# Attention with a bucketed position bias and a gated feed-forward block on one core: another opening (turns as plain products, one-step bias table, bias rows in 16 copies, another order)

## The chip, the cores and the metric

The kernel runs on one core of one Trainium2 chip. The core has five engines with an instruction queue each: TensorE (PE, matrix products into PSUM), VectorE (DVE), ScalarE (ACT), GpSimd (POOL) and SyncE (SP, which here only issues transfers). ACT and POOL issue transfers as well. All transfers share 16 DMA engines. PSUM has 8 banks of 128 x 512 fp32. The metric is device time in microseconds (us), lower is better.

## The reference

Inputs are q, k, v of shape 8 x 8 x 576 x 64 (batch, heads, positions, head size), a bias table of 32 x 8, and a feed-forward layer with w_in 512 x 2048, w_out 2048 x 512 and alpha 2048, all fp32. What is computed:

```
scores = q k^T / 8 + bias_table[bucket(|i - j|)]     # one bias per head and distance
attn   = softmax(scores);   x = (attn v), heads side by side: 4608 x 512
h = x w_in;   s = sin(alpha h);   g = h + s*s / (alpha + 1e-9);   out = g w_out
```

The bucket is the distance itself below 16, grows with its logarithm up to 31, and is 31 for every far distance.

## The kernel before, in words

Work goes batch by batch (t = 0 to 7). For each batch the scores are made transposed, keys on partitions: two heads of a pair share a product, four blocks of 128 keys (units "A", 128 x 1024 each) and a last 64 keys (unit "C"); the last 64 queries are units "B" and "X", which for batch 0 are done beside batch 1. ACT takes exp(scores / 8) from PSUM into the tile u (L707). The bias is not added but multiplied in afterwards, as exp(bias): since exp of the bias of the last bucket is a common factor that the softmax cancels, the table is taken relative to its last row, and then only a band of some 384 queries around each block of keys needs the product (DVE, L738, by the tile m2r; the C units by mhr, L724). After that u is multiplied by v with a column of ones beside it (products with v and vh), DVE divides by the sums (L952, L953), the result is turned on PE (L1024) and copied to xT, the input of the feed-forward layer. There 16 blocks of 128 columns go through w_in, sine (ACT, L1068), square (ACT L1075 or DVE L1077) and the sum (DVE, L1082) into g; products with w_out follow, and are used to fill PE where the next batch's scores wait for ACT. ACT loads another function table between exponentials and sines (L1146).

The order of instructions on each engine is made when the program is built, by a list planner written in the kernel (class Plan): each task has a priority, an estimated length per engine and sometimes an earliest time (the constants T_...), and the planner emits tasks in the order in which its own clock would run them. On the chip only that order counts; engines wait for each other by semaphores. Where the planner sees PE idle early on, it puts in products of a tile of zeros (zz).

The opening is special. For batch 0, q and k are loaded in their own layout: pair 0 of heads into nat0 (SP, fp32, cast to natb by DVE and POOL, L467, L515, L516), pairs 1 to 3 into nat1 (POOL, cast on the way). They are turned on PE by transposes with the identity (L550, L556: 6 or 12 of 96 columns for one of k or q of one pair) into one PSUM bank as fp16, and copied by DVE into kT and qT (L539). The last 64 keys are copied once more into kt by POOL (L581).

The bias rows are made in the same stretch (plan_table): a fp32 product with a matrix that subtracts the last row of the table (less, L592), its exponential (tabE, L595), a product with the 0/1 bucket constant phi (8 x 512), a copy to e_sb (L605), a transfer of e_sb to DRAM in 5 copies (e_dram, L606), and reads of these back into the 128 partitions, each shifted by one element: m2r in three transfers (2, 2 and 4 heads), mhr in two.

v of batch 0 comes in two ways: heads 0, 1 and 4 to 7 in fp32 by SP into a corner of w_out's tile, cast by POOL (L422); heads 2, 3 and the last 64 keys by POOL's own casting transfers (L414, L426). POOL then issues w_in (four transfers, each two of four row blocks of half the columns; a copy of one element of m2r, named tick, makes it wait for the last band), q and k of batch 1 (nat2), w_out, and v of batch 1.

Of the kernel before, what the change touches and what calls it, by code (L numbers as in the profile page):

```python
# [36 lines left out]
PAIRS = ((0, 1), (2, 3), (4, 5))  # L37
BANKS = {"h": (0, 1, 2, 3, 4, 5), "av": (6, 7), "mo": (7, 6)}


class Task:
    def __init__(self, engs, emit, deps, pri, nb=0.0):
# [5 lines left out]
        self.pad = ()  # L48
# [9 lines left out]
class Cell:  # L58
    v = None


class Plan:
# [31 lines left out]
    def pick(self, b, taken):  # L94
        sets = PAIRS if b.tag == "sc" else [(k,) for k in BANKS[b.tag]]
# [53 lines left out]
    def run(self, t0):  # L149
        free = {e: t0 for e in ("PE", "ACT", "DVE", "POOL", "SP")}  # L150
        todo = list(self.tasks)
        while todo:
# [33 lines left out]
            if e == "PE" and WARM_FROM < free[e] < WARM_END and st > free[e] + WARM_GAP:  # L186
                if self.fill(free[e], 192):
                    free[e] += 0.083
                    continue
# [15 lines left out]
            for n in t.pad if fin < WARM_END else ():  # L205
                self.fill(fin, n)
# [4 lines left out]
WARM_END = 22.0  # L211
# [3 lines left out]
T_START = 4.0  # L215
SPLIT = {0: 3, 1: 3}
PRI_S = 0
T_WI = 16.8
T_TAB = 5.2
T_CL = 24.5  # L220
T_FIRST = (4.75, 5.95)
T_PAIR = ((7.9, 8.5), (9.3, 10.2), (11.6, 12.3))
T_ACT = ()
T_M2 = (13.0, 14.8, 16.0, 16.0)
T_MH = 14.2
T_RST = 25.0
T_V0 = (5.8, 6.4, 8.9, 9.6)
T_P3 = 7.0
T_VA = (10.5, 11.0)
T_VB = (19.5, 19.5, 19.5, 19.5)  # L230
T_AL = (10.0, 560)
LATE = 100
GA = 0.1
# [8 lines left out]
T_V = ((15.5, 19.0), (50.0, 50.0))  # L242
T_TR1 = (36.0, 39.0)
T_W = (25.5, 30.5)
T_WO = (40.5, 43.0, 45.7, 48.3)
WARM0 = 8
WARM1 = 2
WARM_LAG = 0.3
WARM_GAP = 0.12
WARM_FROM = 7.3  # L250
AV_PRI = 400
NORM_PRI = 200
CP_PRI = 0
SIN_SET = "trig_and_small"
# [15 lines left out]
def kernel(  # L270
# [26 lines left out]
    NE = 5  # L297
# [12 lines left out]
    for x in range(EW - 1):  # L310
        phi_np[bt[abs(x - 255)], x] = 1.0
    last_np = np.eye(NB, dtype=np.float32)
    last_np[NB - 1] -= 1.0
    phi_h = nc.inline_tensor(np.concatenate([phi_np, last_np.view(np.float16)], axis=1), "phi_const")
# [16 lines left out]
        "p (h c d) -> p h c d", h=H, c=4)  # L331
    zz = sgl.tile([128, 512], F16, name="zz")
# [5 lines left out]
    tabE = sgl.tile([NB, H], F16, name="tabE")  # L338
    phi_x = sgl.tile([NB, EW + 2 * NB], F16, name="phi_sb")
    phi_sb, less_last = phi_x[:, 0:EW], phi_x[:, EW : EW + 2 * NB].bitcast(F32)  # L340
# [72 lines left out]
    def load_vh(t, h):  # L413
        nc.gpsimd.dma_start(  # L414
            out=vs[t][:, :, h, 0:D], in_=v[t, h, 0:512].rearrange("(c p) d -> p c d", p=128)
        )

    def load_v32(h):
        nc.sync.dma_start(out=vst[:, h], in_=v[0, h, 0:512].rearrange("(c p) d -> p c d", p=128))

# [809 lines left out]
```

## Time and profile before

Three runs took 372.21, 372.88 and 376.88 us (median 372.88). The profiled execution is one more; its own time is given only as its span, from the first to the last instruction.

| | profiled execution before |
|---|---|
| span | 374.9 us (run time around it not shown) |
| PE busy | 368.2 us (98%) |
| ACT busy | 315.7 us (84%) |
| DVE busy | 257.8 us (69%) |
| POOL busy | 91.9 us (25%) |
| first exponential on ACT | 9.11 us |
| first sine | 34.98 us |
| first product with w_out | 49.79 us |

A row of the timeline gives the start, the length, the engine, the line, the operation with its tiles (written <- read), its shape and how many were merged; in brackets stands the idle time before it and what ended it. "issue" means that nothing in the profile explains the wait. A busy PE is not PE at its best: the products of zeros count as busy, and so does a product that runs slowly. Rows of transfers give the number, the KB of each and the median us from issue to landing.

### The profile page before, as it was taken

To read this page: it belongs to the slowest core of one execution; us is meant where nothing else is said; L and a number is where in the kernel's file an instruction comes from. 1 tells how busy PE (TensorE), PEld (TensorE's weight loads), DVE (VectorE), ACT (ScalarE), POOL (GpSimd) and SP (SyncE) were. 2 spreads that over 40 slices of the span, in tenths; PEclk is the share of its full clock that TensorE was granted. 3 is DMA by queue.
4 is the path that set the end of the run, shared out by engine and by line. 5 is a ranking of instruction groups with operands and counts; after the bars stand their busy time and mean duration, and the time that the engine had idled before them with its cause. 6 is when DMAs were issued, how large, how long until landed. Compare 5 with 4: busy or idle time off the path is not lost.

```text
span 374.9 us, 8925 instructions
## 1 busy us (share of the span) xinstructions
PE 368.2 (98%) x3576; PEld 197.4 (53%) x3576; DVE 257.8 (69%) x559; ACT 315.7 (84%) x431; POOL 91.9 (25%) x133
## 2 busy tenths in 40 slices
PE   8999999999999999999999999999999999999996
PEld 3455454644455455684564455444576455444443
DVE  3496976759676967597758867786759675879000
ACT  2787989979997999899989999799979997999211
POOL 7368270037000640055002800090006000000000
PEclk9999999999999999999999999999999999999999
DMA  9969999369922998199917992699249121000112
GB/s 168 201 113 192 200 173 160 83 112 112 133 64 62 151 143 123 48 160 137 133 48 134 125 168 58 122 88 187 59 111 118 65 58 47 7 27 5 73 69 85
DMA packets 149114, 40.49 MB, mean 108 GB/s; under 512 B 137080, under 2 KB 143568, under 8 KB 149072
## 3 DMA queue, kind: packets, MB, share of 16 engines
q0 software_dynamic: 96032, 17.67, 58.3%
q1 hardware_dynamic: 52864, 22.16, 24.6%
q8 instruction: 28, 0.46, 0.5%
q10 hardware_dynamic: 176, 0.09, 0.1%
q14 instruction: 14, 0.11, 0.1%
HBM read 37.73 MB, written 16.56 MB: 145 GB/s over the span
## 4 chain that ended last, share of the span: by engine, by line
PE 95%; ACT 3%; DVE 1%; issue 0%; ACTq 0%
PE pb L457 92%; ACT u L707 3%; PE pb L556 2%; PE pb L1024 1%; PE pb L550 0%; DVE xn L953 0%; DVE u L738 0%; DVE qT L539 0%; DVE zz L508 0%; ACT outs L537 0%; ACT xT L537 0%; DVE rd L952 0%; PE pb L646 0%; PE pb L934 0%; ACTq L537 0%
## 5 line engine op out<-in xcount | busy, mean ns | idle before, releaser
L707 ACT ACTIVATE u<-pb 128x1024 f16<-128x1024 f32 (+1 forms) x146 | 137.4, 1017 | 11.9 <-PE pb L457 10.5
L457 PE MATMUL pb<-w_out,g 128*128 128x512 f16 (+2 forms) x592 | 139.0, 374 | 0.0
L457 PE MATMUL pb<-xT,w_in 128*128 128x512 f16 (+4 forms) x704 | 127.4, 340 | 0.0
L1082 DVE SCALAR_TENSOR_TENSOR g<-sq,inv_a,pb 128x512 f16<-128x512 f16 x144 | 101.3, 744 | 7.1 <-PE pb L457 2.7
L1068 ACT ACTIVATE s<-pb,alphaT 128x512 f16<-128x512 f32 x144 | 92.9, 692 | 12.4 <-PE pb L457 11.9
L457 PEld LDWEIGHTS <-w_in 128*128 128x128 f16 x704 | 64.6, 98 | 57.4
L457 PEld LDWEIGHTS <-g 128*128 128x128 f16 x592 | 53.9, 98 | 60.2 <-issue 5.6
L738 DVE TENSOR_TENSOR u<-u,m2r 128x512 f16<-128x512 f16 (+1 forms) x128 | 62.3, 493 | 33.6 <-ACT u L707 31.9
L457 PEld LDWEIGHTS <-u 128*128 128x128 f16 x1152 | 43.4, 97 | 9.6 <-issue 4.6
L402 POOL COPY kt<-kT 64x256 f16<-64x256 f16 x12 | 4.9, 410 | 172.0 <-DMA kT<-staged_k 107.8
L457 PE MATMUL pb<-qT,kT 64*128 64x64 f16 (+1 forms) x512 | 43.3, 293 | 1.1 <-ACT u L707 0.6
L1075 ACT ACTIVATE sq<-s 128x512 f16<-128x512 f16 x69 | 43.1, 637 | 1.2 <-DVE g L1082 0.3
L457 PE MATMUL pb<-v,u 128*128 128x65 f16 x1024 | 43.7, 193 | 0.0
L1077 DVE TENSOR_TENSOR sq<-s 128x512 f16<-128x512 f16 x75 | 30.9, 422 | 12.5 <-ACT s L1068 11.7
L953 DVE TENSOR_TENSOR xn<-pb,rd 128x256 f16<-128x256 f32 (+2 forms) x59 | 28.5, 483 | 2.0
L457 PEld LDWEIGHTS <-kT 64*128 64x128 f16 x512 | 16.2, 95 | 23.1 <-issue 16.8
L457 PE MATMUL pb<-vh,u 128*128 128x130 f16 x128 | 28.2, 221 | 0.0
L407 POOL DMA_DIRECT2D v<-in_v_dram x28 | 24.8, 900 | 4.0 <-DMA nat<-in_k_dram 2.1
L537 ACT ACTIVATE outs<-pb 128x512 f32<-128x512 f32 (+2 forms) x12 | 6.9, 572 | 19.9 <-PE pb L457 19.9
L952 DVE RECIPROCAL rd<-pb 128x4 f32<-128x4 f32 (+2 forms) x59 | 11.0, 186 | 13.3 <-PE pb L457 13.1
L539 DVE COPY outs<-pb 128x512 f32<-128x512 f32 x25 | 17.2, 686 | 4.1 <-PE pb L457 4.1
L1146 ACT ACT_TABLE_LOAD x15 | 19.2, 1283 | 0.3
(75 smaller groups left out, 192.5 us busy)
## 6 DMA issues: line engine op xcount, KB each, us to landing
out_dram<-outs SPq DMA_DIRECT2D x35, 256.0 KB, 2.8
v<-in_v_dram POOLq DMA_DIRECT2D x28, 128.0 KB, 4.6
staged_k<-in_k_dram POOLq DMA_DIRECT2D x6, 576.0 KB, 8.9
staged_q<-in_q_dram POOLq DMA_DIRECT2D x6, 576.0 KB, 12.1
w_in<-in_moe_w_in_dram POOLq DMA_DIRECT2D x4, 512.0 KB, 8.5
w_out<-in_moe_w_out_dram POOLq DMA_DIRECT2D x4, 512.0 KB, 14.5
w_out<-in_v_dram SPq DMA_DIRECT2D x6, 128.0 KB, 5.7
xT<-xn SPq DMA_TRANSPOSE x47, 2.4
```

The lines of the kernel that those rows point to most:

```text
L407: nc.gpsimd.dma_start(out=vs[t % 2][:, c, :, 0:D], in_=vp[128 * c : 128 * c + 128],)
L457: nc.tensor.matmul(out=out, lhsT=lhsT, rhs=rhs, start=start, stop=stop)
L539: k_of(e).tensor_copy(out=o, in_=i)
L707: nc.scalar.activation(out=o, in_=x, func=AF.Exp, scale=0.125)
L738: nc.vector.tensor_tensor(out=io, in0=io, in1=m2[:, 2 * p : 2 * p + 2, x0 : x0 + hi - lo], op=ALU.mult)
L952: nc.vector.reciprocal(out=r, in_=x[:, :, :, D])
L953: nc.vector.tensor_tensor(out=xn[:, 0:n].rearrange("p c (z d) -> p c z d", z=2), in0=x[:, :, :, 0:D], in1=r.unsqueeze(3).to_broadcast([128 ...
L1068: nc.scalar.activation(out=s16.v, in_=h.v, func=AF.Sin, scale=alphaT[:, f : f + 1])
L1075: nc.scalar.activation(out=sq.v, in_=s16.v, func=AF.Square)
L1077: k_of(e).tensor_tensor(out=sq.v, in0=s16.v, in1=s16.v, op=ALU.mult)
L1082: nc.vector.scalar_tensor_tensor(out=gcell[b].v[:, f, :], in0=sq.v, scalar=inv_a[:, f : f + 1], in1=h.v, op0=ALU.mult, op1=ALU.add,)
L1146: nc.scalar.preload_act_table_set(name)
```

## The change

All of it concerns batch 0 and the loads around it.

- The turns of batch 0 become plain matrix products with the identity. Their result is fp32 and takes two PSUM banks (three blocks of 96 columns in each), from four possible bank pairs of which three are those of the scores. DVE copies out of the two banks.
- The table: DVE splits the fp32 table into two fp16 parts (tab16), before its casts of q and k; two products with phi add up the parts, and phi itself carries the -1 for the last row. ACT takes the exponential straight from PSUM into e_sb. The fp32 product and its exponential are gone.
- e_sb is written to DRAM in 16 copies instead of 5; a band (m2r) is read head by head, eight transfers, partitions spread over the copies in groups of 8.
- nat0 is loaded in halves, one head each, on SP and on ACT; phi and alpha move from ACT's queue to SP's. The last cast of q of pair 0 moves from POOL to ACT.
- v: all heads and the last 64 keys now come in fp32 by SP and are cast by POOL.
- POOL's queue: w_in in three transfers by columns (a quarter, a quarter, a half), after the casts of v of heads 2, 3 and 4 and without the tick; then the other casts, q and k of batch 1, and w_out after all casts.
- Zeros: 7 products of 512 and 6 of 128 columns at the start, and fewer later; other times and lengths in the planner, and a table of priorities (HEAD_PRI) for the first tasks.

The order that results: PE makes the turns of pair 0, then both turns of pair 1, then the first two score units. On SP stand, after the first loads: bands 0 and 1, the two of mhr, bands 2 to 7, v of heads 2 to 7. In the feed-forward block of batch 0, 48 products with w_in stand before the first turn of batch 1 (40 before), and 12 products with w_out before the first scores of batch 1 (17 before). Later batches are ordered much as they were.

```diff
-    last_np = np.eye(NB, dtype=np.float32)
-    last_np[NB - 1] -= 1.0
-    phi_h = nc.inline_tensor(np.concatenate([phi_np, last_np.view(np.float16)], axis=1), "phi_const")
+    phi_np[NB - 1, 0 : EW - 1] -= 1.0
+    phi_h = nc.inline_tensor(phi_np, "phi_const")
...
-    load_nat(nat0[:, 0], 0, 2, k[0], nc.sync)
-    load_nat(nat0[:, 1], 0, 2, q[0], nc.sync)
     nc.scalar.dma_start(out=tabN, in_=bias_table)
-    nc.scalar.dma_start(out=phi_x, in_=phi_h.ap())
-    nc.scalar.dma_start(out=alphaN, in_=moe_alpha.rearrange("(f p) -> f p", p=128))
+    for kq, src in ((0, k), (1, q)):
+        for z, eng in ((0, nc.sync), (1, nc.scalar)):
+            load_nat(nat0[:, kq, z : z + 1], z, z + 1, src[0], eng)
+    nc.sync.dma_start(out=phi_sb, in_=phi_h.ap())
+    nc.sync.dma_start(out=alphaN, in_=moe_alpha.rearrange("(f p) -> f p", p=128))
     load_v32(0)
     load_v32(1)
+    load_vt32()
...
-    cast0(0, nc.vector)
-    x0 = nat0[:, 1].rearrange("s two (i d) -> s i two d", i=SI)
-    nc.vector.tensor_copy(out=natb[:, 1, :, 0], in_=x0[:, :, 0])
-    P_.tensor_copy(out=natb[:, 1, :, 1], in_=x0[:, :, 1])
+    nc.vector.tensor_copy(out=tab16[:, 0], in_=tabN)
+    nc.vector.tensor_tensor(out=tab16[:, 1], in0=tabN, in1=tab16[:, 0], op=ALU.subtract)
+    x0 = nat0.rearrange("s kq two (i d) -> s kq i two d", i=SI)
+    for kq, z in ((0, 0), (0, 1), (1, 0)):
+        nc.vector.tensor_copy(out=natb[:, kq, :, z], in_=x0[:, kq, :, z])
+    nc.scalar.activation(out=natb[:, 1, :, 1], in_=x0[:, 1, :, 1], func=AF.Copy)
...
         def mm(e):
+            if t == 0:
+                c.v = bank(b, 2)
+                for i in range(SI):
+                    o = c.v[:, i // 3, SN * (i % 3) : SN * (i % 3) + SN]
+                    if p == 0:
+                        full(o, natb[:, kq, i], id_sb[0:SN, 0:SN], True, True)
+                        continue
+                    for z in range(2):
+                        full(o[64 * z : 64 * z + 64], nat1[:, kq, 2 * p - 2 + z, D * i : D * i + D],
+                             id_sb[0:SN, 0:SN], True, True)
+                return
...
+        def mm(e):
+            for x in range(2):
+                full(bank(b)[0:H, 0:EW], tab16[:, x], phi_sb, x == 0, x == 1)
 
         def ex(e):
-            nc.scalar.activation(out=tabE, in_=bank(a)[0:NB, 0:H], func=AF.Exp)
...
+            nc.scalar.activation(out=e_sb, in_=bank(b)[0:H, 0:EW], func=AF.Exp)
+            nc.scalar.dma_start(out=e_dram.ap()[:, 0:H].rearrange("r h x -> h r x"),
+                                in_=e_sb.unsqueeze(1).to_broadcast([H, NE, EW]))
+            load_m2r(0, 2)
             load_mhr(nc.sync)
...
+    def load_m2r(h0, h1):
+        n = 128 // NE
+        for h in range(h0, h1):
+            nc.sync.dma_start(
+                out=m2r[:, h],
+                in_=bass.AP(tensor=e_dram, offset=EW * h, ap=[[4 * H * EW + n, NE], [1, n], [1, XW]]),
+            )
...
-        def w_in(e):
-            P_.tensor_copy(out=tick, in_=m2r[0:1, 4, 0:1])
-            for hf in range(2):
-                load_w_in16(hf, (0, 2))
...
+        for h in range(H):
+            vdone.append(plan.add({"POOL": 0.45}, lambda e, h=h: cast_v(h), [], 9010 + h, nb=T_V0[h]))
...
+        x = vdone[2]
+        for i, (x0, x1) in enumerate(((0, 1), (1, 2), (2, 4))):
+            x = plan.add({"POOL": 0.85}, lambda e, x0=x0, x1=x1: load_w_in16(x0, x1), [], 9012.5 + i,
+                         nb=T_WI + 0.8 * i, after=[x])
+        x = plan.add({"POOL": 1.7}, lambda e: load_nat2(), [], 9021, nb=T_RST, after=[x])
+        x = plan.add({"POOL": 3.2}, lambda e: load_w_out16(), [], 9022, nb=T_WL, after=[x] + vdone)
...
+    for i, x in HEAD_PRI.items():
+        plan.tasks[i].pri = x
     plan.run(T_START)
```

More of the change, by code (lines that the diff above doesn't have):

```diff
@@ L149, in run @@
     def run(self, t0):
-        free = {e: t0 for e in ("PE", "ACT", "DVE", "POOL", "SP")}
+        free = dict(t0)
         todo = list(self.tasks)
@@ L611, in cp, with bands @@
+            load_m2r(0, 2)
             load_mhr(nc.sync)
[L612 to L614 removed]
+        def bands(e):
+            load_m2r(2, H)
+            for h in range(2, H):
                 load_v32(h)
[L617 to L618 removed]
+        x = plan.add({"PE": D_TAB}, mm, [], -1100, nb=T_PHI, new=[b])
+        y = plan.add({"ACT": 1.1}, ex, [x], -1100, use=[b])
@@ L726, in bd @@
                 )
-            d = plan.add({"POOL": 0.45} if t == 0 and p else {"DVE": 0.25 if two else 0.15}, bd, [x],
+            d = plan.add({"POOL": 0.6} if t == 0 and p else {"DVE": 0.25 if two else 0.15}, bd, [x],
                          base + 10, nb=late, use=[ub])
```

177 lines of the change are left out of this document (77 added, 100 removed), and 10 rows, old and new, of the table HEAD_PRI.

## The prediction

> **What bounds the kernel now.** I read the summary page first: the span and the chain that ended last.
>
> ```profile
> span 374.9 us, 8925 instructions
> PE 95%; ACT 3%; DVE 1%; issue 0%; ACTq 0%
> ```
>
> PE holds 95% of the chain, so later work moves earlier only if the opening (the first 51 us, which the diff rewrites) hands it over earlier. A busy PE says little there, because part of its work is products of zeros and part runs slowly. The timeline shows the pace:
>
> ```profile
> 1.27 3.92 PE L457 MATMUL pb<-zz 128*128 128x512 f16 x10 [1.27 <-DVE zz L508]
> 33.92 7.50 PE L457 MATMUL pb<-xT,w_in 128*128 128x512 f16 x34
> 19.08 0.39 PE L457 MATMUL pb<-zz 128*128 128x256 f16 x1
> 20.80 0.30 PE L457 MATMUL pb<-zz 128*128 128x256 f16 x1
> 8.47 0.61 PE L457 MATMUL pb<-qT,kT 64*128 64x512 f16 x2 [0.37 <-DVE qT L539]
> 21.13 0.39 PE L457 MATMUL pb<-qT,kT 64*128 64x512 f16 x2
> 11.15 0.69 PE L556 MATMUL pb<-id_sb,nat 96*64 96x96 f16 x12
> 41.35 0.45 PE L556 MATMUL pb<-id_sb,nat 96*64 96x96 f16 x12
> ```
>
> The first row is eight products of 512 columns and two of 192: 4480 columns in 3.92 us, 1.14 per ns. The second is 17408 in 7.50 us, 2.32 per ns. The same zero product falls from 0.39 to 0.30 us between 19.08 and 20.80, a score pair from 0.61 to 0.39, twelve turns from 0.69 to 0.45. In this execution PE ran at half pace until about 20.8 us. What that costs is read on ACT:
>
> ```profile
> 9.11 1.02 ACT L707 ACTIVATE u<-pb 128x1024 f16<-128x1024 f32 x1 [1.46 <-PE pb L457]
> 30.62 1.28 ACT L1146 ACT_TABLE_LOAD   x1
> 34.98 1.84 ACT L1068 ACTIVATE s<-pb,alphaT 128x512 f16<-128x512 f32 x3 [0.48 <-PE pb L457]
> 50.70 1.28 ACT L1146 ACT_TABLE_LOAD   x1
> 54.84 6.78 ACT L707 ACTIVATE u<-pb 128x1024 f16<-128x1024 f32 x7 [0.64 <-PE pb L457]
> ...
> L707 ACT ACTIVATE u<-pb 128x1024 f16<-128x1024 f32 x16 | 15.6, 1039 | 4.6 <-PE pb L457 4.6
> L707 ACT ACTIVATE u<-pb 128x512 f16<-128x512 f32 x4 | 2.4, 610 | 0.7 <-PE pb L457 0.7
> ```
>
> The last two rows group the twenty exponentials between 9 and 31 us (after the bar: busy time and mean ns of one; idle time before them and who ended it). After the first one ACT waits 4.6 + 0.7 - 1.46 = 3.84 us for PE. It reaches the sine at 34.98 and leaves feed-forward block 0 at 50.70 (second table load). Third, the transfers:
>
> ```profile
> 20.00:22.50 2.50, 2.47 (x38) 1.33 (x33) 2.50 (x7) 2.45 (x3) 2.41 (x5) 1.00 0.00 0
> 21.28 2.92 POOL L438 DMA_DIRECT2D w_in<-in_moe_w_in_dram  x4
> nat<-in_q_dram POOLq DMA_DIRECT2D x1, 576.0 KB, 10.0
> 32.13 0.78 POOL L432 DMA_DIRECT2D nat<-in_q_dram  x1
> 42.69 0.31 PEld L556 LDWEIGHTS <-nat 96*64 96x64 f16 x12 [0.42 <-issue]
> ```
>
> In the windows view the last two columns are DMA share and GB/s: nothing moves from 20.0 to 22.5, then w_in starts a queue (w_in, next batch's k and q, w_out, v) without a gap. Its q lands at 32.13 + 10.0 = 42.1, and PE begins turning it at 42.69, 0.6 later. So the start of w_in, W = 21.28, is a second chain beside ACT's: q at W + 20.8.
>
> **The change part by part.** *Turns.* As many products as before, into fp32, two PSUM banks instead of one. Why the pace rose at 20.8 no row says; the stretches before it had the same kinds of product with waits between (0.37 ahead of 8.47), and the new order sets more products back to back. If PE is at full pace when the exponentials begin, twelve cost 0.45 instead of 0.69, and a turn with a score pair 0.45 + 0.39 = 0.84 us, under an exponential's 1.02; at half pace it is 1.30, over it. The copy out now reads fp32:
>
> ```profile
> L539 DVE COPY qT<-pb 128x576 f16<-128x576 f16 x4 | 3.0, 755 | 3.1 <-PE pb L556 2.0 <-PE pb L550 1.1
> L539 DVE COPY outs<-pb 128x512 f32<-128x512 f32 x25 | 17.2, 686 | 4.1 <-PE pb L457 4.1
> ```
>
> The fp32 row scales to 0.686 x 576/512 = 0.77 us against 0.755: eight times 0.02, nothing. The extra banks can hold up a score pair: between 0 and one copy, 0.77; I take 0, since the exponentials leave a bank pair every 1.02. One bound of the other kind, a gain, is excluded: no copy gets shorter.
>
> The Trainium skill's "TensorE: Matmul & The Clock Gate" (Part 4) says that transpose-mode products do not count as PE-busy for the clock's release. Here 24 turns at 17.98 to 19.15 stood in the stretch after which the pace rose, so the trace neither bears this out nor excludes it. By that rule and the page's 3.4 us window, plain products would bring the release by about 8 us, an estimate; without it the half pace may last, which is a rival below.
>
> *Opening order.* Two turns of pair 1 now precede the first scores, so these wait for its q (issued 2.29, below; landing 6.1: 8.4). Turn 0.45 to 0.69 and scores 0.39 to 0.61 put the first exponential at 9.3 to 9.7 instead of 9.11; I take +0.4. Three xT copies instead of one now stand on ACT before the table load (+0.76), and fewer after it. The exponentials end at 30.62 - 3.84 + 0.40 + 0.76 = 27.9.
>
> *Table.* The fp32 subtraction and its exponential go, two tiny DVE operations and a second 512-column product come.
>
> ```profile
> 2.29 0.64 POOL L432 DMA_DIRECT2D nat<-in_q_dram  x1
> nat<-in_q_dram POOLq DMA_DIRECT2D x3, 144.0 KB, 6.1
> phi_sb<-phi_const ACTq DMA_DIRECT2D x1, 36.0 KB, 4.0
> 6.44 0.58 PE L457 MATMUL pb<-phi_sb,tabE 32*8 32x512 f16 x1
> 7.06 0.59 ACT L605 ACTIVATE e_sb<-pb 8x512 f16<-8x512 f32 x1 [0.67 <-PE pb L457]
> 7.68 0.52 ACTq L606 DMA_DIRECT2D e_dram<-e_sb  x1
> 10.28 0.37 SPq L473 DMA_DIRECT2D m2r<-e_dram  x1
> 10.69 1.34 SPq L480 DMA_DIRECT2D mhr<-e_dram  x2
> m2r<-e_dram SPq DMA_DIRECT2D x2, 192.0 KB, 4.4
> mhr<-e_dram SPq DMA_DIRECT2D x2, 96.0 KB, 4.3
> w_out<-in_v_dram SPq DMA_DIRECT2D x6, 128.0 KB, 5.7
> ```
>
> The constant is third on SP (about 1.7) and lands at 1.7 + 4.0 = 5.7; products of 0.43 + 0.58 end at 6.7, and e_sb starts 0.3 us earlier than 7.06. The write grows from 40 to 128 KB. Written and acknowledged it took 10.28 - 7.68 = 2.6; the bounds are that and the 4.3 of a 96 KB landing. I take 2.9, which eats the 0.3: the first band read stays at 10.3. The Trainium skill's "DMA: Bandwidth & Descriptors" (Rules for kernel authors) says that a transfer whose outermost dimension is under 16 uses no more engines than that; this write is outermost over 8 heads, so the rule speaks for the upper bound, by which the first band read goes 1.4 later, at 11.7, and W with it. Separate copies may make the reads faster than 4.4, or eight pieces slower; bounds 2.6 to 5.7, taken 4.3. The multiplies then begin at about 14.5 instead of 17.14:
>
> ```profile
> 17.14 0.41 DVE L738 TENSOR_TENSOR u<-u,m2r 128x512 f16<-128x512 f16 x1
> 32.93 0.42 DVE L953 TENSOR_TENSOR xn<-pb,rd 128x256 f16<-128x256 f32 x1
> ```
>
> DVE had waited 3.1 us for PE before the q copies alone (row above); its last normalisation ends at 33.35; started 2.6 earlier it ends near 30.7, in step with ACT's 30.62 - 27.9 = 2.7. The sine starts at 34.98 - 2.7 = 32.3.
>
> *v and w_in.* Four v transfers move from POOL to SP, whose queue becomes: band 0, 1, the two mhr, bands 2 to 7, then v of heads 2 to 7. POOL no longer waits for the bands before w_in, but for the cast of head 2 (row below). Queued behind that cast: all of w_in, the next k and q, w_out.
>
> ```profile
> 25.69 1.09 POOL L422 CAST v<-w_out 128x256 f16<-128x256 f32 x3
> ```
>
> Head 2 is issued at 10.3 + 0.37 + 0.37 + 1.34 + 6 x 0.37 = 14.6 and lands 4.3 (as mhr) to 5.7 (as v) later; I take 4.3, because POOL's own v traffic in those microseconds is gone. With a 0.4 cast W = 19.3, 2.0 earlier. Quarters of w_in arrive in the order of use, for nothing: the sine does not wait for them (first half of w_in is there before PE begins it at 32.5). q lands at 19.3 + 20.8 = 40.1.
>
> *Sum.* The first turn of the new batch comes after 48 w_in products instead of 40, two feed-forward blocks more.
>
> ```profile
> L1068 ACT ACTIVATE s<-pb,alphaT 128x512 f16<-128x512 f32 x144 | 92.9, 692 | 12.4 <-PE pb L457 11.9
> L1075 ACT ACTIVATE sq<-s 128x512 f16<-128x512 f16 x69 | 43.1, 637 | 1.2 <-DVE g L1082 0.3
> ```
>
> A block costs ACT one sine and 69/144 of a square, 0.69 + 0.31 = 1.0 us. Before, PE came to the turn 41.35 - 34.98 = 6.4 after the sine; now it is there at 32.3 + 6.4 + 2.0 = 40.7, just after q. From q's turn (42.69) to the table load (50.70) it was 8.0: 48.7, a gain of 2.0. Then 12 instead of 17 w_out products stand before the first scores of batch 1, which ends ACT's wait of 0.64. From there the two orders agree: 374.9 - 2.0 - 0.6 = 372.3.
>
> That stands on the profiled span. The runs gave 372.21, 372.88 and 376.88, so this execution lies between them and 2.0 above the median; what the run time holds around the span is not shown. I read the two low runs as openings in which PE's pace rose earlier. Part of the gain is then in the median already: the forecast is 0.6 below it, not 2.6.
>
> **The rivals.** *The median had the slow opening too* (the span is longer for being profiled): the whole 2.6 comes off 372.88, 370.3. For it: only three runs; against it: 376.88.
>
> *The half pace stays.* If zeros, or the narrow 8-column table products, hold the release back to 20 us as before, a turn and a pair cost 1.30 and the waits remain at about 0.3 per exponential for eight of them, 2.4 of the 3.84. Less the later start, the gain is near 0.5 on this span: 374.4. Against it: the new order leaves PE fewer gaps.
>
> *v gates w_in, slower.* If the bands land in 5.7, SP cannot issue v of head 2 at 14.6: in the changed instruction list the later bands and the v's each wait for the transfer eight places before them. Band 6 then waits for band 0's landing, 10.3 + 5.7 = 16.0, and two issues of 0.37 later head 2 goes at 16.8, lands at 22.5, W = 22.9; q at 43.7, the table load at 51.7, 1.0 late, less the 0.6: 375.3 by the same sum, 2.4 above the median. It decides from W = 21.28 on: past it the new order gives POOL's queue a later start than the old one. Against it: the 0 GB/s window shows that the old transfers were through by 20.0, and the new ones are about as many bytes.
>
> **How the numbers follow.** Forecast 372.3: 0.46. Median slow too, 370.3: 0.22. v gates: 0.20. Half pace stays: 0.12. The bank and copy bounds (0.77) and the landing bounds (1.4 either way) widen these: 368.8 to 375.4. A run of this kernel tells 2% (7.5 us) from no change; no case reaches it, so faster 0.03, within 0.94, slower 0.03.
>
> **What would show it.** Right: score pairs of 0.39 by 10 us; ACT's waits after the first exponential under 1 us in all; first band multiply near 14.5; first w_in issue near 19.3; first sine near 32; second table load near 48.7. Wrong: pairs of 0.61 past 15 us; w_in issued after 21.3; turns of the new batch waiting for a landing; or a second load earlier than 47.

## The result and the profile after

The changed kernel took 374.82 us (median of 20 runs, 373.93 to 376.27), the kernel before beside it 372.95 (20 runs, 372.21 to 376.88). The ratio is 1.0039, with a 95% interval of 1.002 to 1.0058: slower by 0.4%, some 1.5 us (the two medians lie 1.9 apart). It lies inside the predicted range, but above the kernel before, where the forecast of 372.3 lay below it.

The kernel before has two levels (of 135 runs in all comparisons 116 lie at 374.9 or below and 18 between 376.2 and 377.8), so its median is one of the lower level; four disturbed runs above 382 us, one of before and three of one experiment, are left out.

The profiled execution of the changed kernel took 374.36 us and has a span of 372.7. Of the page, the span and the shares of the chain that ended last:

```profile
span 372.7 us, 8932 instructions
PE 88%; DVE 3%; ACT 3%; DMA 3%; issue 1%; SPq 1%; ACTq 0%; DVEq 0%
```

PE has 88% of the chain, where it had 95%; DMA, DVE and SP's queue have come into it. The timeline after (start, length, engine, line, operation, idle time before it and who ended that) has the rows that answer to those of before:

```profile
7.51 0.53 ACTq L629 DMA_DIRECT2D e_dram<-e_sb  x1
9.94 10.25 ACT L728 ACTIVATE u<-pb 128x1024 f16<-128x1024 f32 x12 [2.45 <-PE pb L478]
10.60 0.39 PE L478 MATMUL pb<-qT,kT 64*128 64x512 f16 x2
11.55 1.20 SPq L496 DMA_DIRECT2D m2r<-e_dram  x2
14.10 4.09 SPq L496 DMA_DIRECT2D m2r<-e_dram  x6
15.39 0.71 DVE L758 TENSOR_TENSOR u<-u,m2r 128x768 f16<-128x768 f16 x1 [0.74 <-DMA m2r<-e_dram]
18.23 3.34 SPq L431 DMA_DIRECT2D w_out<-in_v_dram  x6
19.98 0.42 PE L478 MATMUL pb<-v,u 128*128 128x65 f16 x8 [1.02 <-DVE u L758]
21.31 2.66 ACT L728 ACTIVATE u<-pb 128x512 f16<-128x512 f32 x3 [1.12 <-PE pb L478]
21.42 0.40 POOL L444 CAST v<-w_out 128x256 f16<-128x256 f32 x1 [3.91 <-DMA w_out<-in_v_dram]
21.76 0.81 POOL L459 DMA_DIRECT2D w_in<-in_moe_w_in_dram  x1
22.30 0.61 PE L478 MATMUL pb<-qT,kT 64*128 64x512 f16 x2
24.71 3.45 ACT L728 ACTIVATE u<-pb 128x1024 f16<-128x1024 f32 x4 [0.73 <-PE pb L478]
32.72 1.84 ACT L1088 ACTIVATE s<-pb,alphaT 128x512 f16<-128x512 f32 x3 [0.48 <-PE pb L478]
48.58 1.28 ACT L1166 ACT_TABLE_LOAD   x1
51.96 6.55 ACT L728 ACTIVATE u<-pb 128x1024 f16<-128x1024 f32 x7
```

The first sine (the start of feed-forward block 0 on ACT) is at 32.72 instead of 34.98 and the second table load at 48.58 instead of 50.70: against the profile of before, the changed kernel is 2.2 us ahead, close to the 2.6 of the sum. The score pairs take 0.39 us at 10.60; the ACT wait of 0.64 ahead of batch 1 is gone (51.96). Yet the measured time is 1.9 above the median of before. So the question is not where the gain went in this profile, but which execution of before the profile shows.

What is new in the opening is in the chain of waits, cut to its first 36 us (start, length, what):

```profile
7.51 4.02 DMA e_dram<-e_sb
...
14.75 3.35 DMA m2r<-e_dram
...
19.98 3.59 PE pb L478 x48
```

The chain runs through the write of the bias rows to DRAM (4.02), SP's issues of the reads behind it, the read of band 2 (3.35) and the first multiplications, to 48 products, most of them of v and u, among which the next scores stand in PE's queue. PE waits 1.02 there, and the exponential behind it 1.12. In the profile of before the chain in these microseconds was PE itself at half pace, up to ACT's exponentials from 20.05 on:

```profile
18.05 1.10 PE pb L556 x24
```

### The profile page after: what moved, and what is told of

The parts are those of the page before. It is cut to its first block, busy times and chain, and to the rows that moved or that the text cites. A ratio compares the mean times of both kernels' runs of the same rounds, so it can differ in the third digit from the quotient of the medians.

```text
span 372.7 us, 8932 instructions
## 1 busy us (share of the span) xinstructions
PE 364.2 (98%) x3569; PEld 196.9 (53%) x3569; DVE 259.3 (70%) x560; ACT 316.7 (85%) x433; POOL 88.6 (24%) x130
## 3 DMA queue, kind: packets, MB, share of 16 engines
q1 hardware_dynamic: 54432, 22.30, 25.4%
## 4 chain that ended last, share of the span: by engine, by line
PE 88%; DVE 3%; ACT 3%; DMA 3%; issue 1%; SPq 1%; ACTq 0%; DVEq 0%
PE pb L478 87%; DVE u L758 1%; DMA e_dram<-e_sb 1%; DVE g L1102 1%; ACT u L728 1%; DMA natx<-in_k_dram 1%; DMA m2r<-e_dram 1%; PE pb L1044 1%; ACT nat L728 1%; SPq L496 0%; DVE sq L1097 0%; DVE xn L973 0%; ACT qT L563 0%; ACT L1166 0%; SPq L503 0%
## 5 line engine op out<-in xcount | busy, mean ns | idle before, releaser
L758 DVE TENSOR_TENSOR u<-u,m2r 128x512 f16<-128x512 f16 (+1 forms) x128 | 63.1, 497 | 36.4 <-ACT u L728 33.6
L478 PEld LDWEIGHTS <-u 128*128 128x128 f16 x1152 | 44.4, 99 | 11.8 <-issue 5.3
L478 PE MATMUL pb<-v,u 128*128 128x65 f16 x1024 | 44.9, 195 | 1.0 <-DVE u L758 1.0
L1095 ACT ACTIVATE sq<-s 128x512 f16<-128x512 f16 x71 | 44.1, 636 | 1.2 <-DVE g L1102 0.3
L478 PE MATMUL pb<-qT,kT 64*128 64x64 f16 (+1 forms) x512 | 42.5, 288 | 1.8 <-ACT u L728 1.2
L563 ACT ACTIVATE outs<-pb 128x512 f32<-128x512 f32 (+2 forms) x10 | 5.5, 554 | 19.9 <-PE pb L478 19.9
L565 DVE COPY outs<-pb 128x512 f32<-128x512 f32 x27 | 18.5, 686 | 3.8 <-PE pb L478 3.8
```

Of the source, the lines that this page charges most:

```text
L478: nc.tensor.matmul(out=out, lhsT=lhsT, rhs=rhs, start=start, stop=stop)
L565: k_of(e).tensor_copy(out=o, in_=i)
L758: nc.vector.tensor_tensor(out=io, in0=io, in1=m2[:, 2 * p : 2 * p + 2, x0 : x0 + hi - lo], op=ALU.mult)
L1095: nc.scalar.activation(out=sq.v, in_=s16.v, func=AF.Square)
```

## The experiments

Fifteen experiments ran; two of them are the unedited kernels again and one is a repeat. Each was compared with runs of the kernel before on the same chip; the median of before was 373.2, 373.3, 373.2 and 373.2 us in the four groups. Two numbers recur: the time, and when the first sine of feed-forward block 0 starts. Over all 17 profiles the span less that start is 339.5 to 340.6 us (before 374.9 - 34.98 = 339.9; after 372.7 - 32.72 = 340.0), so all but some 1 us of what the change and the experiments do happens ahead of the first sine.

### The kernel before once more

No edit; another profile.

> The kernel before, unchanged, for a second profiled execution. Theory 1 (the profiled execution of before, span 374.9, was an unusually slow opening; the usual one reaches full pace early): a span near 371.2, score pairs of 0.39 us before 10 us, ACT's waits for PE after the first exponential under 1.5 us, w_in issued near 19 and the second table load near 47. Theory 2 (before opens like this each time, and the run time holds less around the span): span 373 to 375 again with pairs of 0.61 past 15 us.

Measured: 373.43 us (372.6 to 376.68), ratio 1.0008 [0.9983, 1.0034]. The profiled execution took 373.51 with a span of 371.6. From its timeline:

```profile
8.17 10.89 ACT L707 ACTIVATE u<-pb 128x1024 f16<-128x1024 f32 x12 [1.21 <-PE pb L457]
19.28 2.92 POOL L438 DMA_DIRECT2D w_in<-in_moe_w_in_dram  x4
31.40 1.84 ACT L1068 ACTIVATE s<-pb,alphaT 128x512 f16<-128x512 f32 x3 [0.48 <-PE pb L457]
47.11 1.28 ACT L1146 ACT_TABLE_LOAD   x1
```

The twelve exponentials from 8.17 take 10.89 us without a wait among them, the sine comes at 31.40 instead of 34.98. Its chain goes through the write and the read, as in the changed kernel:

```profile
7.00 3.73 DMA e_dram<-e_sb
...
10.80 4.08 DMA m2r<-e_dram
```

So the same program has openings in which PE is at full pace early (six turns take 0.34 us at 5.05 here, 0.48 at 5.18 in the first profile), and others in which it is at half pace until 20.8. The profile that the prediction used is one of the second kind. The profiled executions whose own time is known took 1.7 to 1.9 us more than their span, this one and the changed kernel's among them. Twelve runs of before have the very span of 374.9, and they took 376.7 to 376.9; so the execution that the prediction used took, by an estimate from these, some 376.8, the upper level of the runs.

### 5 copies instead of 16

```diff
-    NE = 16
+    NE = 5
...
         for h in range(h0, h1):
+            rr = (0, 0, 3, 3, 4, 4, 4, 4)[h]
...
-                in_=bass.AP(tensor=e_dram, offset=EW * h, ap=[[4 * H * EW + n, NE], [1, n], [1, XW]]),
+                in_=bass.AP(tensor=e_dram, offset=EW * (4 * H * rr + h), ap=[[1, 128], [1, XW]]),
```

> The changed kernel with the bias rows in 5 copies instead of 16, read head by head from one copy each as the old kernel did. Theory A (the bigger write delays the first band read, 11.55 instead of 10.3, and with it all of SP's queue, v of head 2 and w_in): first band read near 10.2, w_in issued near 20.4 instead of 21.8, time 1.0 to 1.5 us under the changed kernel's. Theory B (16 copies pay by faster reads, and the loss lies in the order of POOL's queue): reads of a band take over 4 us instead of 3.0, w_in no earlier than 21.5, time the same or 0.5 longer.

Measured: 373.38 us (372.77 to 375.31), ratio 1.0009 [0.9995, 1.0024].

```profile
6.79 0.52 ACTq L629 DMA_DIRECT2D e_dram<-e_sb  x1
10.01 0.88 SPq L496 DMA_DIRECT2D m2r<-e_dram  x2
18.80 0.56 PE L478 MATMUL pb<-v,u 128*128 128x65 f16 x8 [0.94 <-DVE u L758]
31.40 1.84 ACT L1088 ACTIVATE s<-pb,alphaT 128x512 f16<-128x512 f32 x3 [0.48 <-PE pb L478]
```

The first band read is issued 3.22 us after the write (4.04 in the changed kernel), the products of v and u start 1.2 earlier, the sine 1.3 earlier, at the very 31.40 of the kernel before at full pace. The 16 copies with their spread reads are the loss; the rest of the change taken together moves nothing that these runs can tell from zero.

### w_in ahead of v

```diff
+        def v_cast(h):
+            if h == 2:
+                for x0, x1 in ((0, 1), (1, 2), (2, 4)):
+                    load_w_in16(x0, x1)
+                load_nat2()
+            cast_v(h)
```

w_in and the next k and q are issued by POOL ahead of the cast of head 2 instead of behind the casts of heads 2 to 4.

> The changed kernel with w_in and the next batch's k and q issued by POOL ahead of the cast of v of head 2 instead of behind it; the order on the other engines is unchanged. Theory A (w_in behind v of head 2 is what binds block 0 of the feed-forward): w_in issued near 17.5, next batch's q landing near 38 instead of 41, time 1 to 2.5 us under the changed kernel's. Theory C (the transfers are shared, so w_in in front slows v and the bands, and block 0 is bound by ACT): first sine no earlier or later than 32.7, time within 0.5 of the changed kernel's.

Measured: 390.03 us (389.36 to 391.06), ratio 1.0453 [1.043, 1.0476]. Neither theory had this.

```profile
18.80 2.30 POOL L459 DMA_DIRECT2D w_in<-in_moe_w_in_dram  x3
19.73 14.76 SPq L431 DMA_DIRECT2D w_out<-in_v_dram  x6
29.68 0.40 POOL L444 CAST v<-w_out 128x256 f16<-128x256 f32 x1 [7.02 <-DMA w_out<-in_v_dram]
49.23 1.84 ACT L1096 ACTIVATE s<-pb,alphaT 128x512 f16<-128x512 f32 x3 [0.48 <-PE pb L478]
```

w_in goes out 3.0 us earlier, at 18.80, and then SP needs 14.76 us for the six issues of v that took 3.34, the cast of head 2 comes at 29.68 instead of 21.42, and the sine at 49.23. With POOL's casting transfers under way, SP's small loads beside them hardly moved here. The wait of w_in behind v, which the prediction costed as a loss, protects v.

### Transposes again, in fp16 and one bank

```diff
-                c.v = bank(b, 2)
+                c.v = bank(b, 2)[:, 0, :].bitcast(F16)
...
-                        full(o, natb[:, kq, i], id_sb[0:SN, 0:SN], True, True)
+                        nc.tensor.transpose(out=o, in_=natb[:, kq, i], identity=id_sb[0:SN, 0:SN])
```

The same for the pairs from nat1.

> The changed kernel with the turns of batch 0 as transposes again (fp16 into one bank of the pair), same order. Theory D (plain products are what brings the full pace early): pairs of 0.61 until 15 us or later, time 1 to 3 us over the changed kernel's. Theory E (transposes count as well, the pace depends on how closely the products follow): full pace at the same 10 us, time within 0.5 of the changed kernel's.

Measured: 374.91 us (374.18 to 376.14), ratio 1.004 [1.0014, 1.0065]: the changed kernel's own time.

```profile
5.09 0.43 PE L577 MATMUL pb<-id_sb,natx 96*128 96x96 f16 x6 [0.34 <-DVE natx L542]
9.19 0.45 PE L580 MATMUL pb<-id_sb,nat 96*64 96x96 f16 x12
9.57 0.39 PE L478 MATMUL pb<-qT,kT 64*128 64x512 f16 x2
18.05 0.61 PE L478 MATMUL pb<-qT,kT 64*128 64x512 f16 x2
```

With transposes among the first products, twelve turns take 0.45 and a score pair 0.39 us by 9.6: full pace. Already the first six transposes, at 5.09, take 0.43 us (0.69 at half pace, at 4.98 in the first profile of before). So the pace had risen behind the products of zeros that stand ahead of them, and the run doesn't tell whether transposes can raise it. Here the plain products buy nothing, and the second bank costs nothing. A fall to 0.61 at 18.05 comes here as in the changed kernel (0.61 at 22.30).

### 16 copies alone, in the kernel before

```diff
-    NE = 5
+    NE = 16
...
-        eng.dma_start(
-            out=m2r[:, h0:h1],
-            in_=bass.AP(tensor=e_dram, offset=EW * (4 * H * r + h0), ap=[[1, 128], [EW, h1 - h0], [1, XW]]),
-        )
+        n = 128 // NE
+        for h in range(h0, h1):
+            eng.dma_start(
+                out=m2r[:, h],
+                in_=bass.AP(tensor=e_dram, offset=EW * h, ap=[[4 * H * EW + n, NE], [1, n], [1, XW]]),
+            )
```

> The kernel before with one part of the change alone: bias rows written in 16 copies, each band read head by head with the partitions spread over the copies. Theory "copies cost" (the 128 KB write is acknowledged later, and w_in, which waits here for band 4 by the tick, goes later by as much): the first band read about 4.0 to 4.4 us after the write instead of 2.6 to 3.8, the first w_in 0.5 to 1.5 us after the 19.3 of the kernel before's new profile, and the time 0.5 to 1.5 us above the kernel before. Rival "copies cost only together with v on the bands' queue" (in the changed kernel v of heads 2 to 7 stands behind the bands): here the time stays within 0.3 us of the kernel before.

Measured: 376.40 us (nine runs, 375.06 to 377.00), ratio 1.0052 [1.0013, 1.0091]. Three of the runs lie at 375.1 to 375.5, six at 376.4 to 377.0, where before has its upper level; all lie above every run of before's lower level beside them (the highest is 374.79). The copies cost in the old order too, so the second theory falls; the size is above what the first expected. The profiled execution (376.4) has a half-pace opening, and shows nothing of the cost:

```profile
7.68 0.52 ACTq L608 DMA_DIRECT2D e_dram<-e_sb  x1
11.85 1.26 SPq L475 DMA_DIRECT2D m2r<-e_dram  x2
17.13 0.41 DVE L740 TENSOR_TENSOR u<-u,m2r 128x512 f16<-128x512 f16 x1
34.96 1.84 ACT L1070 ACTIVATE s<-pb,alphaT 128x512 f16<-128x512 f32 x3 [0.48 <-PE pb L457]
```

The band read goes out 4.17 us after the write instead of 2.60, and first multiplication and sine stand where they stood in the profile of before (17.14, 34.98). At half pace the bias rows have at least 1.6 us of slack, and an experiment that is read from such an execution finds the copies free. How many of the nine runs had that opening is not known, so the size at full pace isn't settled by this kernel.

### Merged band reads

The 5-copy version with the three reads of before.

```diff
+        if h0 == 0:
+            parts = ((0, 2, 0),)
+        else:
+            parts = ((2, 4, 3), (4, 8, 4))
+        for a0, a1, rr in parts:
...
+                out=m2r[:, a0:a1],
+                in_=bass.AP(tensor=e_dram, offset=EW * (4 * H * rr + a0), ap=[[1, 128], [EW, a1 - a0], [1, XW]]),
```

> The changed kernel with 5 copies and the three merged band reads of before (2, 2 and 4 heads) instead of eight. If the number of transfers ahead of v on SP matters, v of head 2 is issued about 1.5 us earlier (three issues instead of eight), w_in goes out near 18.5 to 19.5 instead of 20.05, and the time is 0.3 to 0.8 us below the version with 5 copies and eight reads (373.4). Rival: the bands' bytes and not their issues set when v lands, w_in stays near 20 and the time at 373.4 within 0.3; the first multiplies may wait longer for a merged read.

> The version with 5 copies and merged band reads once more, on the chip of these runs: 373.0 to 373.6 again, 1.2 to 1.8 below the changed kernel beside it; if the earlier run was luck of that chip, 374 or more.

Measured: 373.30 us (371.43 to 374.59), ratio 0.996 [0.9922, 0.9997]; a second time 372.79 (372.04 to 374.65), ratio 0.9989 [0.9975, 1.0002]. The first ratio is flattered: 9 of the 35 runs of before beside it were on the upper level. The issue of v began at 13.71 and 13.26, 2.6 and 3.0 us ahead of the version with eight reads (16.26), but the cast of head 2 came only 0.4 and 1.1 earlier, at 19.34 and 18.57 (19.71). So most of the gain in issues is lost again before v has landed; that the bands' bytes ahead of v are the reason, as the rival has it, is argued, not shown. In the times, the first run fits the rival (373.4 within 0.3) and the second the first theory (w_in at 19.14, 0.6 below 373.4), so the two runs leave it open whether merging pays.

### Zeros put back

```diff
+            for n in t.pad if fin < WARM_END else ():
+                self.fill(fin, n)
...
+            m.pad = (256,) if p else ()
```

The 5-copy version with eight reads, with 256 columns of zeros after turns and score units of batch 0.

> The version with 5 copies, with products of 256 columns of zeros put back after the turns and score units of batch 0, as in the kernel before. Theory "the clock's relapse costs" (the changed opening leaves PE more gaps, and its pace falls back between 12 and 22 us): no relapse in this run, and a time 0.3 to 0.8 us below 373.4. Rival "the relapse is free, ACT or the loads set the pace there": 373.4 within 0.3, or slower by the zeros' own time.

Measured: 375.16 us (374.02 to 376.05), ratio 1.0014 [0.998, 1.0048], 1.9 above the merged version on the same chip. Its fastest run was the profiled one, with the sine at 31.96. The products still fell back to half pace (0.61 us for two of 256 columns at 15.23, 0.54 for a score pair at 17.65), so the zeros did not remove this relapse, and the run can't tell what the relapse costs; it tells that the zeros, with the order that the planner makes around them, cost.

### Without the table of priorities

```diff
-    for i, x in HEAD_PRI.items():
-        plan.tasks[i].pri = x
```

> The version with 5 copies without the table of priorities for the first tasks (the order is then the planner's own). If the searched order is worth something, the first exponential or the sine is later by 0.5 us or more and the time 0.5 to 1.0 us above 373.4; rival: the order of the first tasks is covered by the loads (q of batch 1 lands at the same time), and the time stays at 373.4 within 0.3.

Measured: 374.74 us (373.68 to 376.41), ratio 1.0015 [0.9978, 1.0052], 1.4 above the merged version on the same chip. Here, too, the profile is of the fastest run. Its sine, at 32.36, is 1.0 later than with the searched order (31.40). The order is worth 1.0 to 1.4 us, the one part of the change for which a gain of its own was seen.

### The changed kernel again, and v of heads 2 and 3 ahead of the later bands

```diff
-            load_m2r(2, H)
-            for h in range(2, H):
+            load_v32(2)
+            load_v32(3)
+            load_m2r(2, H)
+            for h in range(4, H):
                 load_v32(h)
```

> The changed kernel unedited, beside the next runs on one chip. Theory (the 16-copy write and w_in behind v of head 2 cost about 1.4 us): 374.5 to 375.2, w_in near 21.8, 1 to 2 us above the kernel before's openings at full pace (about 373.0).

> The changed kernel, 16 copies and eight reads kept, with v of heads 2 and 3 issued on SP ahead of bands 2 to 7 instead of behind them. Theory "the loss is w_in's late start behind v": the cast of head 2 stops waiting for a load, w_in goes out 2 to 4 us earlier (near 18 to 19.5) and the time falls by about 1.4 us, to 373.4. Rival "the loss is the bands' late landing itself (first multiplies at 15.4)": the bands land another 0.5 us later and the time stays at 374.8 or goes above it. Third: w_in, started while bands and v of heads 4 to 7 are still queued, starves them, and the time goes above 376.

Measured: the changed kernel 374.69 us (374.5 to 375.22), ratio 1.0037 [1.0018, 1.0055]; the moved one 379.53 (378.84 to 379.92), ratio 1.0165 [1.0144, 1.0186].

```profile
18.25 0.81 POOL L459 DMA_DIRECT2D w_in<-in_moe_w_in_dram  x1
21.38 0.62 PE L478 MATMUL pb<-v,u 128*128 128x65 f16 x8 [2.40 <-DVE u L760]
30.15 0.28 PE L478 MATMUL pb<-v,u 128*128 128x65 f16 x4 [1.70 <-POOL v L444]
```

w_in goes out 3.5 us earlier than in the changed kernel (18.25 against 21.76), the sine comes at 37.33, and the kernel is 4.8 us slower. My theory that the loss is w_in's late start falls. The second and the third expectation both came true: the bands land later (PE waits 2.40 for the multiplication, 1.02 in the changed kernel), and v of head 4, behind w_in, reaches its product at 30.15.

The same move on top of 5 copies and merged reads:

> 5 copies, merged band reads, and v of heads 2 and 3 ahead of the later bands. If both causes add up, w_in near 17.5 to 18.5 and a time 0.5 to 1.0 us below the version without the move (373.3), thus below both kernels. Rival: PE or ACT sets the pace once w_in is out by 20, and the time stays within 0.3 of 373.3; starved bands would put it above 374.

Measured: 374.34 us (372.9 to 375.56), ratio 1.0018 [0.9993, 1.0044], 1.55 above the same kernel without the move, on the same chip (372.79): above 374, as the last of the expectations had it.

```profile
17.81 0.81 POOL L459 DMA_DIRECT2D w_in<-in_moe_w_in_dram  x1
31.80 1.84 ACT L1093 ACTIVATE s<-pb,alphaT 128x512 f16<-128x512 f32 x3 [0.48 <-PE pb L478]
```

From this sine to the second table load it is 15.9 us, as in the changed kernel (48.58 - 32.72) and in the kernel before at full pace (15.7), although w_in was issued 14.0 us ahead of the sine here, 11.0 there, 12.1 there. In none of these does q of batch 1 hold that stretch up: the second chain through w_in binds nothing here.

### The write and the reads apart

Three versions with the three merged reads, differing in the copies (NE) and in which of them is read:

```diff
-    NE = 5
+    NE = 16
```

and NE = 3 and NE = 1, with the reads from copies 0, 1, 2 or all from copy 0.

> The changed kernel with its 16 copies written, but the bands read as before in three transfers, each from one copy. If the larger write is the cause: write to first band read 4.0 to 4.4 us against 3.5 to 3.6 with 5 copies and the same reads, first sine 0.5 to 0.9 later than there (31.0 and 31.6), time 0.5 to 1.0 us above 373.0. If the single, spread reads are the cause: time within 0.3 of 373.0, although the write is larger.

> 3 copies (24 KB) and three merged reads. If the price goes with the size of the write: 3.0 to 3.3 us from the write to the first band read, the sine 0.2 to 0.5 earlier than with 5 copies and the time 372.5 to 372.9. Rival: the write's fixed part sets it, no change from 373.0.

> One copy (8 KB), all reads from it. If the price goes with the size: 2.6 to 3.0 us from the write to the first band read and a time of 372.0 to 372.6. Rival: the partitions' overlapping reads of one copy collide, the bands land later than the 3.9 to 4.1 us of 5 copies, and the time stays at 373 or above.

| copies, band reads | time, us | ratio to before, interval | write to first band read, us | first sine, us |
|---|---|---|---|---|
| 16, eight spread (the change) | 374.82; 374.69 | 1.0039 [1.002, 1.0058]; 1.0037 [1.0018, 1.0055] | 4.04; 4.10 | 32.72; 33.58 |
| 16, three | 373.89 | 1.0008 [0.9983, 1.0034] | 4.57 | 32.66 |
| 5, eight | 373.38 | 1.0009 [0.9995, 1.0024] | 3.22 | 31.40 |
| 5, three | 373.30; 372.79 | 0.996 [0.9922, 0.9997]; 0.9989 [0.9975, 1.0002] | 3.47; 3.62 | 30.97; 31.59 |
| 3, three | 373.42 | 0.9997 [0.9974, 1.0021] | 2.77 | 30.94 |
| 1, three | 373.00 | 1.0001 [0.9975, 1.0026] | 4.07 | 32.84 |

The times are medians, the last two columns one profiled execution each. With three reads the large write costs 0.6 to 1.1 us (373.89 against 373.30 and 372.79); with the large write the eight spread reads cost another 0.8 to 0.9 (374.82 and 374.69 against 373.89). Taken as they stand, both are at work and their sum is the loss. But these differences go across chips, and beside the two kernels of its own chip (3 copies and 1 copy) the large write costs 0.5 and 0.9, less than the intervals can tell from zero. That 16 copies and their reads together are the loss is shown by the version with 5 and eight; how it divides between write and reads is an estimate.

In every profile with 16 copies, seven with the two of the table's first row, the read waits 4.0 to 5.9 us for the write; up to 5 copies it is 2.6 to 4.1. Below 5 copies no further gain is seen, against the first expectation of each: the differences of these three medians are smaller than the intervals, and one copy had 4.07 us in the one execution that was profiled. The waits of 16 copies and of fewer touch there, so from a single profile the wait can't be tied to the size of the write.

The version with 5 copies and three reads beats the changed kernel by 1.9 us on the same chip (372.79 against 374.69, and only 1 of its 12 runs lies above the lowest of the other). Whether it beats the kernel before is not shown: one interval ends below 1, the other at 1.0002.

### What the waiting does to PE's pace

Most of these openings hold a second stretch at half pace. In the windows view (stretch, then length, busy times of PE, PEld, DVE, ACT and POOL, PEclk, DMA share and GB/s) of the changed kernel:

```profile
16.00:20.00 4.00, 2.29 (x14) 0.90 (x14) 3.46 (x9) 4.00 (x6) 1.19 (x3) 1.00 0.72 137
20.00:24.00 4.00, 4.00 (x60) 3.35 (x61) 2.91 (x9) 2.72 (x4) 2.56 (x5) 0.57 1.02 202
```

and of the version with 5 copies and three reads, in its first profile:

```profile
16.00:20.00 4.00, 2.89 (x31) 1.49 (x31) 2.82 (x7) 4.00 (x5) 2.11 (x5) 1.00 1.06 242
20.00:24.00 4.00, 3.71 (x69) 2.65 (x66) 3.90 (x13) 3.40 (x5) 3.98 (x9) 1.00 0.87 138
```

Behind the 48 products that the chain holds stands a turn (of the attention result). In the changed kernel the products start at 19.98, and the turn is the row

```profile
23.38 0.40 PE L1044 MATMUL pb<-id_sb,xn 128*128 128x128 f16 x2
```

In the other kernel the same products and the turn behind them start at

```profile
19.34 0.42 PE L478 MATMUL pb<-v,u 128*128 128x65 f16 x8 [0.51 <-DVE u L761]
21.59 0.27 PE L1047 MATMUL pb<-id_sb,xn 128*128 128x128 f16 x2
```

PE idles 1.7 of the 4 us ahead of the late multiplication, and in the next 4 the granted clock is 0.57; from the first of the 48 products to the turn behind them it is 3.40 us. In the other kernel PE waits 0.51 at that place instead of 1.02, the clock stays at 1.00, and the same stretch is 2.25. So between these two executions the slow products cost 1.15 us, more than the 0.64 by which they start later.

That the wait causes the relapse isn't shown. In the profile with 5 copies and eight reads the clock is down to 0.57 from 12 to 16 us already, ahead of that place, with PE busy for 3.36 us of the 4 before, and the sine still comes at 31.40. Over whole runs, all 27 of the changed kernel have a mean granted clock of 0.995 or less, as have 9 of the 98 runs on the lower level of before whose clock is on record; these 9 are 1.2 us longer than the others in the mean. In the 5-copy version with three reads the runs with the lower clock are 0.8 us longer in one set (373.5 against 372.7) and 0.2 in the other.

So the relapse is a rival to the copies as the cause. The version with 5 copies and eight reads speaks against it: six of its twelve runs have the lower clock, and these six take 373.6 in the mean, 1.3 below the changed kernel's 27 (375.0). With the relapse on both sides the copies still cost; whether the relapse adds to the loss is open.

## Why the prediction was wrong

**The step that failed first is the last one of the sum, "That stands on the profiled span".** It set the span of 374.9 beside the run times 372.21, 372.88 and 376.88 and put the execution between them. All profiled executions of known time took 1.7 to 1.9 us more than their span, and runs of before with this span took 376.7 to 376.9: it was a run of about 376.8, on the upper level, with the half-pace opening. The step did suspect that the low runs have faster openings, but took only 2.0 of distance where it was 3.8. By its own sum, 372.3 of span are 374.0 of run time, already 1.1 above the median. The sum gave nearly the span that was measured (372.7); it answered how far the change goes from a slow opening, and the median has the other.

**The bounds were read from that opening too.** Half pace hid the chain through the bias rows: in before, write and read had at least 1.6 us of slack (16 copies changed nothing there), while at full pace the chain runs through them. The gain that the change was to bring, an ACT that doesn't wait, the median of before has already.

**The write, taken at 2.9 us, took 4.04 (4.10 in the second profile).** This is the mis-sized term of the loss: with it the first band read is at 11.55, not 10.3. The rule of the Trainium skill's "DMA: Bandwidth & Descriptors" (Rules for kernel authors), that an outermost dimension under 16 confines a transfer to at most so many engines, had spoken for the upper bound of 4.3 and, by the prediction's estimate, a read at 11.7. The trace agrees with that time; whether the number of engines is the reason no run here tells, and one copy took 4.07 once.

**The issues of the single bands, 0.37 each, took 0.68** (six in 4.09), and two before them 0.60. That and the write put v of head 2 at 18.23 instead of 14.6. It landed faster than the 4.3 taken (cast at 21.42, 3.2 later), as did the single bands (3.1 us from issue to landing), so W was 21.76, not 19.3.

**The second chain, q at W + 20.8, bound nothing; it came from a row read as the wrong turn.** The row 42.69 of before, read as the turn of q 0.6 us behind its landing, is the second turn of k, as the copies behind the turns show:

```profile
42.20 0.70 ACT L537 ACTIVATE kT<-pb 128x576 f16<-128x576 f16 x1
43.87 0.73 ACT L537 ACTIVATE kT<-pb 128x576 f16<-128x576 f16 x1
45.60 1.24 ACT L537 ACTIVATE qT<-pb 128x576 f16<-128x576 f16 x2
```

q was first turned at 44.90, 2.8 us after it had landed. In the changed kernel it landed at 41.9 (issued at 27.22, 14.7 us), W + 20.1, and its first turn came after 43.28. Over the profiles W moved between 17.8 and 22.0 without touching the stretch from sine to second table load, 15.7 to 15.9 (16.5 only with the zeros put back, where the order in that stretch is another; the kernel with w_in ahead of v is not counted). That the table load came out right (48.58 for 48.7) is the sum of a sine that was 0.4 late and a turn that waited for nothing. The 0.64 of ACT's wait went, but from the table load to the end it is 324.1 us, before 324.2: the gain was given back later. The next two table loads, 75.13 and 93.52 before, are at 72.35 and 90.27, 2.8 and 3.3 ahead; from the one at 171.99 (169.91) on it is 2.1 again. To what it went in between was not looked into.

**Right:** full pace by 10 us (0.39), the first sine near 32 (32.72), the span. The sine was in part luck: the table load ahead of it came at 29.93, not at the 27.9 of the sum, and the stretch between the two shrank from 4.4 to 2.8 us, which the prediction had not forecast. **Nearly:** the first exponential (9.3 to 9.7, 9.94), the first multiplication (14.5, 15.39). **Wrong:** ACT's waits under 1 us (1.12 + 0.73), w_in near 19.3.

**The turns at no cost** were right: as transposes they gave 374.91 against 374.82. The rule of the Trainium skill's "TensorE: Matmul & The Clock Gate" (Part 4), that transposes do not count for the clock, is not tested by that kernel: its pace had risen ahead of its first transposes (0.43 us at 5.09).

**The rivals.** "The median had the slow opening too" is refuted by the second profile of before; "the half pace stays" by the pairs of 0.39. "v gates w_in" gave 375.3 and named the place where the queue was held; its trigger (W past 21.28) came. But its price was that of w_in's late start, and w_in started earlier makes the kernel slower by 4.8 and 15 us. What the runs show to cost stood ahead of v: the bias rows' write and the bands.

**The range** is not what its own terms give: 1.4 either way makes 368.9 of the lowest case, close to its 368.8, but 376.7 of the highest (375.3), not 375.4.

## What to carry to other kernels

Before costing a change, add what lies around the span and see on which level of the runs the profiled execution stands; where the runs have two levels, profile again, because the bound may be another one. Look for the first event after which the rest of the span is constant (here the first sine, 340 us ahead of the end), and follow the chain of waits to that event alone. A round trip through DRAM on that chain is priced by its write and its issues as much as by its reads: here 16 copies of the source went with a longer write, and reading head by head with longer issues.

## What the runs showed of the hardware

- PE's pace in the same program had risen by about 5 us in one execution and rose at 20.8 in another, with some 3.3 us between their run times (373.5, and 376.8 by the estimate above). The clock records don't show the first half-pace stretch: the windows of before from 5 to 20 us have a PEclk of 1.00, and score pairs take 0.61 in them.
- The pace fell back in mid-opening (granted clock 0.57 from 20 to 24 us) behind a stretch in which PE was busy for 2.29 of 4 us; in another kernel it fell as far (0.57 from 12 to 16 us) behind one in which PE was busy for 3.36 of 4.
- With POOL's casting transfers issued 3.0 us earlier, ahead of them, SP's six loads of 128 KB were issued over 14.76 us instead of 3.34, and the kernel took 390 us.
- Single band reads took SP longer to issue (six for six heads in 4.09 us with 16 copies, in 3.99 with 5) than merged ones (1.12 for two transfers that hold the same six heads), and the write of 128 KB was followed by its first read after 4.0 to 5.9 us, of 8 to 40 KB after 2.6 to 4.1.
